# Clustered attention and two MLPs on one core: transposed keys and queries written straight into the score operands, two operand sets by parity

## The chip, the cores and the metric

One core of a Trainium2 chip runs the whole program. The metric is device time in microseconds (us) of one execution; the median of several runs counts. Five engines work side by side and wait for each other through semaphores: TensorE (PE; PEld is its weight load), VectorE (DVE), ScalarE (ACT), GpSimd (POOL), and SyncE (SP), whose queue issues every DMA here, in program order.

## The reference: what is computed

Two batches, eight heads, 768 tokens, head width 64, sixteen centroids per head. A query attends only to the keys that have the same nearest centroid:

```
q_assign = argmax(q_n @ c_n.T)          # per head; q_n, k_n, c_n are normalised
k_assign = argmax(k_n @ c_n.T)
mask   = q_assign[:, None] == k_assign[None, :]
scores = where(mask, scale * q @ k.T, -1e9)
attn   = softmax(scores);  y = attn @ v
x = y as (1536 tokens, 512)
x = (sigmoid(x @ w_gate) * (x @ w_val)) @ w_out      # F1 = 1536
x = relu(x @ w_in2)**2 @ w_out2                      # F2 = 2048
```

The MLP weights come as 64-bit floats and are decoded on the core into a high and a low float32 part.

## The kernel before

Every float32 number is used as a sum of a rounded high part (`hi`) and a rest (`lo`), because TensorE reads rounded operands. The heads are taken two at a time: eight pairs (2 batches by 4), numbered i = 0 to 7. A pair has 12 units: 2 heads (e), 2 halves of the queries (n), 3 blocks of 128 queries (j). So there are N = 96 units, and the main loop runs once per unit n: row maximum of the scores (DVE, L875), exponential (ACT, L896), six transposes of the probabilities of unit n-3 (PE, L776), their high part (ACT, L778) and low part (DVE, L784), the scores of unit n+1 (PE, L758), a third of the product with the values (PE, L794 and L795), and the normalisation of a unit's probabilities (POOL, L829). Engines run their queues in program order.

While the units of one pair run, `prep` makes the operands of the next. Its steps are spread over units by the tables `STEPS` and `SECOND_STEPS` (for pair 1): the key says at which unit of the pair before (0 to 11, negative ones in the pair before that) a step is written. `tk0`, `tk1`, `tq0`, `tq1` transpose half of the keys or queries of both heads (PE, L548) and split the result into `hi` and `lo`; `s0`, `s1`, `b0`, `b1`, `am`, `eq`, `oh`, `on` find the nearest centroids; `mk` makes 16 mask rows for the keys and 16 for the queries of each head; `ka`, `kb`, `qa`, `qb` are `stack`, which brings `hi` and `lo` of one head into the operand of the score product. A step's second part (ACT, DVE, POOL work on the PSUM result) is a "post" that is written early in the next unit.

The score product is two matmuls deep: Q·K = hi·hi + lo·hi in the first (both halves of the 128 rows are used), then hi·lo plus the mask rows in the second (64 + 16 = 80 rows). So a stacked operand needs copies of `hi` and `lo` in other partitions than they were made in, and copies across partitions are DMAs: three per head and tensor, twelve per pair, 192 KB each (L587 to L589). `hi_k`, `lo_k`, `hi_q`, `lo_q` of all pairs but pair 1 lie in pool `hl`, which has one buffer of each; pair 1 borrows a buffer of the attention's own `pt_hi` and `pt_lo`. For queries of pairs 1 to 7 ACT first copies the PSUM result (`full`, L555), then rounds it to `hi` (L556), and POOL subtracts to get `lo` (L557); for keys DVE subtracts straight from PSUM (L560).

The attention's output of a pair is moved across partitions too: two DMAs per head and half, four per half and pair (`x<-oc`, L804 and L805), then POOL adds (L813). After the last unit the MLPs run: blocks of matmuls L342 to L344 and L420, with the decoding of weights on DVE and ACT. Two weights are decoded early, during pairs 0 to 3, in the tile `spare` (`EARLY_PARTS` lists the units).

Of the kernel before, what the change touches and what calls it, by code (L numbers as in the profile page):

```python
# [29 lines left out]
    -9: ["tq0"],  # L30
    -8: ["tk0"],
    -7: ["tk1"],
    -6: ["tq1", "s0"],
    -5: ["load"],
    -4: ["b0"],
    -3: ["s1", "qa"],
    -2: ["ka"],
    -1: ["kb", "qb"],
    0: ["b1"],
    1: ["am"],  # L40
    3: ["eq"],
# [5 lines left out]
    -8: ["tk0", "load"],  # L47
# [3 lines left out]
    -2: ["qa"],  # L51
    -1: ["s1", "b0"],
    0: ["b1", "ka"],
    1: ["kb"],
    2: ["qb"],
    4: ["am"],
# [15 lines left out]
def cluster_attention_two_mlps(  # L72
# [239 lines left out]
    with tc.manual_schedule():  # L312
# [134 lines left out]
        with ExitStack() as ac:  # L447
# [3 lines left out]
            hl = pc.enter_context(tc.tile_pool(name="hl", bufs=1, side="right"))  # L451
# [9 lines left out]
            stk = sc.enter_context(tc.tile_pool(name="stk", bufs=3))  # L461
# [5 lines left out]
            nat_t, ahead = {}, {}  # L467
# [56 lines left out]

            Q, K, V = {}, {}, {}
            factor = {"q": scale, "k": 1.0}

            def prep(i):
# [4 lines left out]
                def transposes(nm, n):  # L533
                    def go():
                        if n == 0 and i == 1:

                            for t, x in ((hi_t, "pt_hi"), (lo_t, "pt_lo")):
                                if x not in ahead:
                                    ahead[x] = ptp.tile([P, NB, NH], F32R, name=x)
                                o = "kq".index(nm) * S  # L540
                                t[nm] = ahead[x].rearrange("p b n -> p (b n)")[:, o : o + S]
                        elif n == 0:
                            hi_t[nm] = hl.tile([P, S], F32R, name=f"hi_{nm}")
                            lo_t[nm] = hl.tile([P, S], F32R, name=f"lo_{nm}")
                        tr = ps_t.tile([P, NH], F32, name="t")
                        src = nat_t[i, nm]
                        for j in range(HB):
                            nc.tensor.transpose(tr[:, j * P : (j + 1) * P], src[:, n * HB + j].rearrange("p h d -> p (h d)"), ident)  # L548

                        def post():  # L550
                            sl = slice(n * NH, (n + 1) * NH)
                            hi, lo = hi_t[nm][:, sl], lo_t[nm][:, sl]
                            if nm == "q" and i > 0:
                                full = am.tile([P, NH], F32, name="full", bufs=1)
                                nc.scalar.activation(out=full, in_=tr, func=AF.Copy, scale=factor[nm])  # L555
                                nc.scalar.copy(hi, full)  # L556
                                nc.gpsimd.tensor_tensor(out=lo, in0=full, in1=f32(hi), op=ALU.subtract)  # L557
                            else:
                                nc.scalar.activation(out=hi, in_=tr, func=AF.Copy, scale=factor[nm])
                                nc.vector.scalar_tensor_tensor(  # L560
                                    out=lo, in0=tr, scalar=factor[nm], in1=f32(hi), op0=ALU.mult, op1=ALU.subtract
                                )

                        return post

                    return go

                def stack_tile(nm, e):
                    if i % 2 == 0 or e == 0:
                        return stk.tile([P, 2, S], F32R, name=f"st_{nm}")  # L570
                    if i < len(pairs) // 2:

                        return x_in[NG - 1][nm == "q"].rearrange("p k t -> p (k t)")[:, : 2 * S].rearrange("p (a s) -> p a s", a=2)
                    if "stk2" not in pools:
                        assert decoded[0] == EARLY and not any(x < N - UPP for x in decoding)
                        early_stack.close()
                        pools["stk2"] = sc.enter_context(tc.tile_pool(name="stk2", bufs=1))
                    return pools["stk2"].tile([P, 2, S], F32R, name=f"st_{nm}")

                def stack(nm, heads=(0, 1)):  # L580
                    def go():
                        for e in heads:
                            t = stack_tile(nm, e)
                            (Q if nm == "q" else K)[i, e] = t
                            t = f32(t)
                            hi, lo = (f32(x[nm][D * e : D * e + D]) for x in (hi_t, lo_t))
# [82 lines left out]
                def mask():  # L669
# [4 lines left out]
                    def post():  # L674
# [8 lines left out]
                        for e in range(0 if i > 0 else 1, 2):  # L683
                            for t, tensor in enumerate((K, Q)):
                                r = slice((2 * t + e) * NCL, (2 * t + e + 1) * NCL)
                                nc.sync.dma_start(out=f32(tensor[i, e][D : D + NCL, 1]), in_=f32(row[r]))
# [3 lines left out]
                if i == 0:  # L690
                    return [
                        transposes("k", 0),
                        transposes("k", 1),
                        transposes("q", 0),
                        transposes("q", 1),
                        stack("k", (0,)),
                        sims(0),
                        sims(1),
                        stack("q", (0,)),
                        back(0),  # L700
                        back(1),
                        argmax,
                        equal,
                        stack("k", (1,)),
                        stack("q", (1,)),
                        onehot,
                        one,
                        mask,
                    ]
# [10 lines left out]
                    "ka": stack("k", (0,)),  # L720
                    "kb": stack("k", (1,)),
                    "qa": stack("q", (0,)),
                    "qb": stack("q", (1,)),
# [26 lines left out]
            DEPTH = (2 * D, D + NCL)  # L750

            def scores(u):
# [3 lines left out]
                for a in range(2):  # L756
                    for m in range(2):
                        nc.tensor.matmul(  # L758
                            st[:, m, :NH],
                            Q[i, e][: DEPTH[a], a, c * P : (c + 1) * P],  # L760
                            K[i, e][: DEPTH[a], a, m * NH : (m + 1) * NH],
# [24 lines left out]
            def attend(i, e, n, third):  # L786
# [9 lines left out]
                if third == 2:  # L796

                    def post():
                        oc = sm.tile([P, NH], F32, name="oc", bufs=2)
# [33 lines left out]
            load(0, "v")  # L833

# [153 lines left out]
```

## Time and profile before

| | |
|---|---|
| median of 3 runs | 851.24 us (849.12 to 852.61) |
| the profiled execution's own time | 852.56 us |
| its span, first to last instruction | 850.8 us |
| mean granted TensorE clock | 0.986 of full speed |
| busy share of the span: PE, DVE, ACT, POOL | 96%, 73%, 53%, 25% |
| last row maximum of the attention (unit 95) starts at | 272.5 us |

The span lies 1.8 us below the time of the same execution; the profiled execution is 1.3 us above the median. "Busy" counts an instruction from its start to its end; PE's instructions overlap, so a busy PE need not be PE at its best.

### The profile page before, as it was taken

What the parts mean: (1) busy time and instruction counts of PE and PEld (TensorE: products, weight loads), DVE (VectorE), ACT (ScalarE), POOL (GpSimd) and SP (SyncE); (2) the same over time, 40 slices, a digit from 0 to 9 for tenths busy, and PEclk for the clock granted to TensorE, in tenths of its full rate; (3) what the DMA queues carried; (4) which work ended last, traced back from release to release, by engine and by line L of the source; (5) the groups of instructions that cost most, each with busy time, mean ns of one, the idle gap of its engine ahead of it and who ended that gap; (6) DMA issues with size and microseconds to landing.
All of it is one profiled execution on the core that took longest, in us unless ns stands there. A gap on an engine that the chain in (4) does not pass through costs nothing.

```text
span 850.8 us, 11707 instructions
## 1 busy us (share of the span) xinstructions
PE 815.1 (96%) x4069; PEld 695.2 (82%) x4069; DVE 622.0 (73%) x1129; ACT 449.5 (53%) x900; POOL 214.6 (25%) x339
## 2 busy tenths in 40 slices
PE   7697899998999999999999999999999999999998
PEld 5587898898989888788888888887878888888886
DVE  5697988898988567765687857796675788688533
ACT  7586888897888323442333213344645642642630
POOL 1567889897788300000000000000000000000000
PEclk9899999999999999999999999999999999999999
DMA  9764845855622212221211212111222212212012
GB/s 197 187 134 124 186 106 138 186 119 125 150 76 59 78 49 75 75 75 49 75 62 63 63 61 75 54 46 50 75 74 75 75 53 74 88 59 74 25 50 99
DMA packets 68107, 75.67 MB, mean 89 GB/s; under 512 B 29680, under 2 KB 56304, under 8 KB 68048
## 3 DMA queue, kind: packets, MB, share of 16 engines
q1 hardware_dynamic: 68048, 74.93, 33.2%
q8 instruction: 32, 0.52, 0.3%
q14 instruction: 27, 0.22, 0.1%
HBM read 45.12 MB, written 3.15 MB: 57 GB/s over the span
## 4 chain that ended last, share of the span: by engine, by line
PE 83%; DVE 5%; ACT 4%; POOL 2%; DMA 2%; issue 2%; SPq 1%; POOLq 0%; ACTq 0%; DVEq 0%
PE bank_b L420 16%; PE bank_a L343 12%; PE bank_a L344 12%; PE bank_a L342 12%; PE bank_a L420 9%; PE s L758 6%; PE t L776 6%; PE o L794 3%; PE o L795 3%; PE t L601 1%; DMA st_q<-lo_q 1%; DVE pt_lo L784 1%; POOL p L829 1%; PE t L548 1%; DMA x_lo<-pt_hi 1%
## 5 line engine op out<-in xcount | busy, mean ns | idle before, releaser
L344 PE MATMUL bank_a<-x_hi,w 128*128 128x512 f32 x480 | 188.5, 393 | 2.1 <-DVE w L230 2.1
L343 PE MATMUL bank_a<-x_lo,w 128*128 128x512 f32 x480 | 190.0, 396 | 0.4 <-POOL x_lo L824 0.4
L342 PE MATMUL bank_a<-x_hi,w 128*128 128x512 f32 x480 | 188.6, 393 | 0.0
L784 DVE TENSOR_TENSOR pt_lo<-t,pt_hi 128x384 fp32r<-128x384 f32 x192 | 97.3, 547 | 23.3 <-ACT pt_hi L778 22.5
L344 PEld LDWEIGHTS bank_a<-x_hi,w 128*128 128x128 f32 x480 | 90.5, 188 | 22.8 <-DVE w L230 2.5
L342 PEld LDWEIGHTS bank_a<-x_hi,w 128*128 128x128 f32 x480 | 90.5, 189 | 21.0
L343 PEld LDWEIGHTS bank_a<-x_lo,w 128*128 128x128 f32 x480 | 90.4, 188 | 20.7 <-POOL x_lo L824 0.8
L386 DVE TENSOR_TENSOR slo<-act,shi 128x512 fp32r<-128x512 f32 x84 | 57.4, 687 | 59.0 <-ACT shi L385 54.5
L829 POOL TENSOR_SCALAR p<-p,nm,ones 128x768 f32<-128x768 f32 x96 | 95.3, 993 | 19.5 <-DVE nm L828 13.1
L776 PE MATMUL t<-ident,p 128*128 128x128 f32 x576 | 83.8, 282 | 15.0 <-POOL lo_q L557 12.8
L875 DVE TENSOR_REDUCE nm<-s 128x1 f32<-128x768 f32 x96 | 90.9, 947 | 4.3 <-PE s L758 4.2
L896 ACT ACTIVATE p<-s,nm 128x768 f32<-128x768 f32 x96 | 88.3, 920 | 7.4 <-DVE nm L828 3.4
L778 ACT CAST pt_hi<-t 128x384 fp32r<-128x384 f32 x192 | 83.6, 488 | 16.3 <-PE t L776 8.7
L776 PEld LDWEIGHTS t<-ident,p 128*128 128x128 f32 x576 | 69.1, 144 | 22.5 <-POOL lo_q L557 13.8
L758 PE MATMUL s<-st_k,st_q 128*128 128x384 f32 (+1 forms) x336 | 81.9, 367 | 2.1 <-ACT p L896 1.1
L420 PE MATMUL bank_b<-wo,shi 128*128 128x512 f32 x256 | 79.3, 390 | 0.5 <-DVE wo L230 0.5
L385 ACT CAST shi<-act 128x512 fp32r<-128x512 f32 x84 | 51.2, 614 | 52.1 <-PE bank_b L420 27.1
L224 ACT CAST w<-wtop 128x512 fp32r<-128x512 f32 x38 | 23.7, 623 | 103.1 <-DVE wtop L242 103.1
L368 DVE TENSOR_TENSOR act<-bank_a,sg 128x512 f32<-128x512 f32 x36 | 24.9, 691 | 66.4 <-PE bank_a L344 60.4
L794 PE MATMUL o<-pt_hi,vt 128*128 128x384 f32 x192 | 66.7, 348 | 0.4 <-ACT oc L800 0.4
L795 PE MATMUL o<-pt_lo,vt 128*128 128x384 f32 x192 | 66.0, 344 | 0.0
L242 DVE SCALAR_TENSOR_TENSOR wtop<-wmag,wbody 128x512 f32<-128x512 f32 x66 | 45.3, 687 | 23.8 <-ACT wmag L210 21.8
(136 smaller groups left out, 1416.7 us busy)
## 6 DMA issues: line engine op xcount, KB each, us to landing
wraw<-in_moe_w_out_dram SPq DMA_DIRECT2D x28, 512.0 KB, 3.3
wraw<-in_moe_w_in_dram SPq DMA_DIRECT2D x16, 512.0 KB, 3.8
x<-oc SPq DMA_DIRECT2D x64, 96.0 KB, 2.7
wraw<-in_moe_w_gate_dram SPq DMA_DIRECT2D x11, 512.0 KB, 3.7
wraw<-in_moe_w_val_dram SPq DMA_DIRECT2D x11, 512.0 KB, 3.6
st_k<-hi_k SPq DMA_DIRECT2D x26, 192.0 KB, 4.1
st_q<-hi_q SPq DMA_DIRECT2D x26, 192.0 KB, 4.1
nat_v<-in_v_dram SPq DMA_DIRECT2D x8, 384.0 KB, 3.2
```

Source lines behind the costliest of these rows:

```text
L342: nc.tensor.matmul(bk, w[:, 0, ks], mov_hi[:, kk], start=(kk == 0), stop=False)
L343: nc.tensor.matmul(bk, w[:, 0, ks], mov_lo[:, kk], start=False, stop=False)
L344: nc.tensor.matmul(bk, w[:, 1, ks], mov_hi[:, kk], start=False, stop=(kk == KD - 1))
L420: nc.tensor.matmul(bk, st, mv, start=(first and n == 0), stop=(last and n == 2))
L758: nc.tensor.matmul(st[:, m, :NH], Q[i, e][: DEPTH[a], a, c * P : (c + 1) * P], K[i, e][: DEPTH[a], a, m * NH : (m + 1) * NH], start=(a == ...
L776: nc.tensor.transpose(tp[:, m, :], Pt[u][:, c * P : (c + 1) * P], ident)
L784: nc.vector.tensor_tensor(out=lo, in0=tp, in1=f32(hi), op=ALU.subtract)
L794: nc.tensor.matmul(o, vt, hi[:, c, :], start=(c == 0), stop=False)
L795: nc.tensor.matmul(o, vt, lo[:, c, :], start=False, stop=(c == NB - 1))
L829: nc.gpsimd.tensor_scalar(out=p, in0=p, scalar1=nm[:, 3:4], scalar2=ones, op0=ALU.mult, op1=ALU.mult)
L875: nc.vector.tensor_reduce(out=nms[n][:, 0:1], in_=st[n][:, :, :NH], axis=AX.XY, op=ALU.max, negate=True)
L896: nc.scalar.activation(out=e.rearrange("p (m n) -> p m n", m=2), in_=st.pop(n)[:, :, :NH], func=AF.Exp, bias=nms[n][:, 0:1], accum_out=nms ...
```

## The change

Transposed keys and queries are written into the operand of head 0 at once; what head 1 and the second halves need is copied from there. The operands are fixed tiles, `stacks[nm, e, x]`, two sets (x = i % 2) instead of rotating buffers. For head 1 the rows are mirrored: its own data stay in the upper 64 partitions, and its mask rows go to partitions 48 to 63 with zeros below (rows 0 to 47, written once), so its second matmul is 128 rows deep instead of 80. Only the low part of the queries has a tile of its own, one buffer for all pairs: a piece of `x_in[2][0]` (`x_hi_65` in listings), from pair 6 on a tile `lo_q` in a new pool.

```
 STEPS = {
-    -9: ["tq0"],  -8: ["tk0"],  -7: ["tk1"],  -6: ["tq1", "s0"],  -5: ["load"],  -4: ["b0"],
-    -3: ["s1", "qa"],  -2: ["ka"],  -1: ["kb", "qb"],  0: ["b1"],  1: ["am"],
+    -8: ["tq0"],  -7: ["tk0"],  -6: ["tk1"],  -5: ["tq1", "s0"],  -3: ["b0", "load"],  -2: ["s1"],
+    -1: ["kb"],  0: ["qb", "b1"],  1: ["am"],  2: ["ka", "qa"],
     3: ["eq"], 6: ["oh", "on"], 7: ["mk"],
...
-    -8: ["tk0", "load"],
+    -8: ["tk0"],
...
-    0: ["b1", "ka"],
+    0: ["b1", "load"],
...
-    4: ["am"],
+    4: ["am", "ka", "qa"],
...
+            stacks[nm, e, x] = stk.tile([P, 2, S], F32R, ...)      # k and q, 2 heads, 2 parities
...
-                        elif n == 0:
-                            hi_t[nm] = hl.tile([P, S], F32R, name=f"hi_{nm}")
-                            lo_t[nm] = hl.tile([P, S], F32R, name=f"lo_{nm}")
+                        if n == 0:
+                            a = stacks[nm, 0, i % 2]
+                            hi_t[nm], lo_t[nm] = a[:, 0], a[:, 1]
+                            if nm == "q":
+                                lo_t[nm] = low_tile()
...
-                            if nm == "q" and i > 0:
-                                full = am.tile([P, NH], F32, name="full", bufs=1)
-                                nc.scalar.activation(out=full, in_=tr, func=AF.Copy, scale=factor[nm])
-                                nc.scalar.copy(hi, full)
-                                nc.gpsimd.tensor_tensor(out=lo, in0=full, in1=f32(hi), op=ALU.subtract)
-                            else:
...
+                            nc.scalar.activation(out=hi, in_=tr, func=AF.Copy, scale=factor[nm])
+                            nc.vector.scalar_tensor_tensor(out=lo, in0=tr, scalar=factor[nm], in1=f32(hi), ...)
+                            if nm == "q":
+                                copy(stacks[nm, 0, i % 2][:D, 1, sl], hi[:D])          # POOL, 64 x 384
+                            if i == 0:
+                                own = stacks[nm, 1, 0][D:, :, sl]
+                                if nm == "q":
+                                    nc.scalar.activation(out=own, in_=tr[D:, None, :].to_broadcast([D, 2, NH]), ...)
+                                else:
+                                    copy(own, stacks[nm, 0, 0][D:, :, sl])
...
-                            nc.sync.dma_start(out=t[:D, 0], in_=hi)
-                            nc.sync.dma_start(out=t[D:, 0], in_=lo if nm == "q" else hi)
-                            nc.sync.dma_start(out=t[:D, 1], in_=hi if nm == "q" else lo)
+                        if e == 0:
+                            nc.sync.dma_start(out=a[D:, 0], in_=f32(lo_t[nm])[:D] if nm == "q" else a[:D, 0])
+                            return
+                        if i > 0:
+                            own = a[D:, 0:1].to_broadcast([D, 2, S]) if nm == "q" else a[D:]
+                            nc.sync.dma_start(out=b[D:], in_=own)
+                        other = f32(lo_t[nm])[D:] if nm == "q" else b[D:, 0] if i == 0 else a[D:, 0]
+                        nc.sync.dma_start(out=b[:D, 0], in_=other)
...
-            DEPTH = (2 * D, D + NCL)
+            DEPTH = ((2 * D, D + NCL), (2 * D, 2 * D))
...
-                            xs[n] = [sm.tile([P, NH], F32, name=f"x{t}", bufs=2) for t in range(2)]
-                        nc.sync.dma_start(out=xs[n][0][own], in_=oc[own])
+                            xs[n] = [oc, sm.tile([P, NH], F32, name="x", bufs=2)]
                         nc.sync.dma_start(out=xs[n][1][own], in_=oc[other])
+                        if e == 1:
+                            nc.sync.dma_start(out=xs[n][0][own], in_=oc[own])
...
+            for nm in "kq":
+                for x in range(2):
+                    nc.gpsimd.memset(stacks[nm, 1, x][: D - NCL, 1].bitcast(I32), 0)
```

What that makes of SP's queue for one pair in the middle (pair 5; `hi_q`, `lo_q`, `hi_k`, `lo_k` are the split transposes, `oc` the attention's output). Before, head 0 (the same six follow for head 1, keys first, then the copies of `oc`):

```order
L587 DMA st_q<-hi_q 64x768
L588 DMA st_q<-lo_q 64x768
L589 DMA st_q<-hi_q 64x768
L587 DMA st_k<-hi_k 64x768
L588 DMA st_k<-hi_k 64x768
L589 DMA st_k<-lo_k 64x768
```

In the changed kernel the same place (`st_k_142` and `st_q_144` are head 0 of this parity, `st_k_143` and `st_q_145` head 1, `x_hi_65` the queries' low part), both heads:

```order
L600 DMA st_k_143<-st_k_142 64x1536
L602 DMA st_k_143<-st_k_142 64x768
L819 DMA x<-oc_2172 64x384
L600 DMA st_q_145<-st_q_144 64x2x768
L602 DMA st_q_145<-x_hi_65 64x768
L596 DMA st_k_142<-st_k_142 64x768
L596 DMA st_q_144<-x_hi_65 64x768
L819 DMA x<-oc_2279 64x384
L821 DMA oc_2052<-oc_2279 64x384
```

Twelve copies of 192 KB became six, two of them of 384 KB; head 1 comes first, since the copies into head 0 (L596) overwrite what head 1's copies read.

DVE's queue at the start, where pair 0's nearest centroids are found (`mx`, `eq`, `m`, `oh`) while pair 1 is split (L560). Before:

```order
L639 TENSOR_REDUCE mx<-tot 128x24
L560 SCALAR_TENSOR_TENSOR pt_lo<-t,pt_hi 128x384
L646 TENSOR_TENSOR eq<-tot,mx 128x384
L649 TENSOR_TENSOR eq<-eq,first 128x384
L560 SCALAR_TENSOR_TENSOR pt_lo<-t,pt_hi 128x384
L656 TENSOR_REDUCE m_313<-eq 128x24
```

In the changed kernel:

```order
L652 TENSOR_REDUCE mx<-tot 128x24
L557 SCALAR_TENSOR_TENSOR x_hi_65<-t,st_q_144 128x384
L659 TENSOR_TENSOR eq<-tot,mx 128x384
L662 TENSOR_TENSOR eq<-eq,first 128x384
L557 SCALAR_TENSOR_TENSOR st_k_142<-t,st_k_142 128x384
L669 TENSOR_REDUCE m_306<-eq 128x24
```

The subtraction ahead of `eq` was one of keys into a borrowed tile; now it is one of queries into the single low tile.

## Rows read from the trace of the kernel before

**Rows 1.** Busy time in stretches: us, each engine's busy us (instructions), clock, DMA share, GB/s.
```profile
30.20:73.61 43.41, 31.83 (x195) 28.89 (x193) 31.15 (x65) 27.22 (x62) 23.60 (x34) 0.92 0.67 159
73.61:106.55 32.94, 30.74 (x202) 29.36 (x201) 29.93 (x61) 27.27 (x64) 28.12 (x41) 0.95 0.62 139
139.37:170.67 31.30, 29.40 (x202) 27.86 (x201) 27.17 (x58) 26.93 (x64) 27.33 (x41) 1.00 0.65 145
170.67:199.64 28.97, 28.73 (x200) 27.61 (x198) 26.49 (x55) 24.98 (x60) 24.88 (x38) 1.00 0.67 148
201.97:230.58 28.61, 28.61 (x189) 27.70 (x188) 25.58 (x53) 25.51 (x61) 23.66 (x37) 0.94 0.55 123
700.00:800.00 100.00, 100.00 (x440) 82.31 (x439) 78.90 (x134) 44.58 (x77) 0.00 (x0) 1.00 0.22 69
```

**Rows 2.** Who waited for whom: us in total, times, longest.
```profile
PE t L776 <- POOL lo_q L557: 12.8, 5, 4.3
ACT hi_q L556 <- DMA st_q<-hi_q: 11.6, 4, 4.6
ACT pt_hi L778 <- DMA x_lo<-pt_hi: 7.0, 1, 7.0
```

**Rows 3.** Timeline around one hand-over (pair 6 ends its copies, pair 7 begins): start, us.
```profile
184.39 0.95 PE L758 MATMUL s<-st_k,st_q 128*128 128x384 f32 x4
188.14 0.48 ACT L800 COPY oc<-o 128x384 f32<-128x384 f32 x1
195.98 0.94 SPq L589 DMA_DIRECT2D st_q<-hi_q  x1
200.10 0.51 ACT L556 CAST hi_q<-full 128x384 fp32r<-128x384 f32 x1 [2.58 <-DMA st_q<-hi_q]
201.73 0.92 PE L776 MATMUL t<-ident,p 128*128 128x128 f32 x6 [2.33 <-POOL lo_q L557]
```

**Rows 4.** Busy time and clock just after another hand-over (columns as in rows 1).
```profile
108.00:110.00 2.00, 2.00 (x10) 1.90 (x9) 1.82 (x4) 1.36 (x3) 1.84 (x4) 0.50 0.00 0
```

**Rows 5.** Groups of instructions by line and shape: count, busy us, mean ns, idle before.
```profile
L557 POOL TENSOR_TENSOR lo_q<-full,hi_q 128x384 fp32r<-128x384 f32 x12 | 12.1, 1004 | 8.5 <-ACT hi_q L556 8.3
L560 DVE SCALAR_TENSOR_TENSOR lo_k<-t,hi_k 128x384 fp32r<-128x384 f32 x14 | 7.6, 549 | 2.7 <-ACT hi_k L559 2.7
L737 POOL TENSOR_SCALAR vt<-nat_v 128x384 fp32r<-128x384 f32 x16 | 8.2, 513 | 1.2
L556 ACT CAST hi_q<-full 128x384 fp32r<-128x384 f32 x12 | 6.2, 513 | 14.2 <-DMA st_q<-hi_q 11.6 <-DMA x_lo<-hi_q 2.4
L795 PE MATMUL o<-pt_lo,vt 128*128 128x384 f32 x192 | 66.0, 344 | 0.0
L758 PE MATMUL s<-st_k,st_q 80*128 80x384 f32 x168 | 44.2, 345 | 1.0 <-issue 0.7 <-ACT st_q L678 0.4
```

**Rows 6.** Issue to landing, of the 192 KB copies L587, then of the 384 KB loads of `nat_v`.
```profile
DMA to landing us min/median/max: 2.6/4.1/6.4
...
DMA to landing us min/median/max: 3.0/3.2/5.8
```

**Rows 7.** The stretch in which the twelve copies of one pair move (columns as in rows 1).
```profile
186.60:200.00 13.40, 12.79 (x88) 12.32 (x87) 11.82 (x25) 10.07 (x24) 10.39 (x17) 1.00 1.00 217
```

**Rows 8.** Timeline of the start: last centroid product, first `eq`, first row maximum.
```profile
10.11 0.37 PE L601 MATMUL t<-lo_q,cen 128*128 128x384 f32 x1
13.38 0.55 DVE L646 TENSOR_TENSOR eq<-tot,mx 128x384 f32<-128x384 f32 x1
20.05 0.96 DVE L875 TENSOR_REDUCE nm<-s 128x1 f32<-128x768 f32 x1 [3.31 <-PE s L758]
```

**Rows 9.** Timeline of the long stall in pair 0, and the row maximum of unit 8 behind it.
```profile
36.08 0.43 DVE L235 TENSOR_SCALAR spare<-spare 128x512 int32<-128x512 int32 x1 [3.49 <-DMA spare<-in_moe_w_gate_dram]
39.87 0.86 ACT L778 CAST pt_hi<-t 128x384 fp32r<-128x384 f32 x2 [6.95 <-DMA x_lo<-pt_hi]
47.35 0.94 DVE L875 TENSOR_REDUCE nm<-s 128x1 f32<-128x768 f32 x1
```

More of the change, by code (lines that the diff above doesn't have):

```diff
@@ L29 @@
 STEPS = {
[L30 to L39, printed above, removed]
+    -8: ["tq0"],
+    -7: ["tk0"],
+    -6: ["tk1"],
+    -5: ["tq1", "s0"],
+    -3: ["b0", "load"],
+    -2: ["s1"],
+    -1: ["kb"],
+    0: ["qb", "b1"],
     1: ["am"],
+    2: ["ka", "qa"],
     3: ["eq"],
@@ L460, in cluster_attention_two_mlps @@
             sc = ac.enter_context(ExitStack())
-            stk = sc.enter_context(tc.tile_pool(name="stk", bufs=3))
+            stacks = {}
+            for x in range(2):
+                stk = pc.enter_context(tc.tile_pool(name="stk0", bufs=1, side="right")) if x == 0 else sc.enter_context(
+                    tc.tile_pool(name="stk1", bufs=1)
+                )
+                for nm in "kq":
+                    for e in range(2):
+                        stacks[nm, e, x] = stk.tile([P, 2, S], F32R, name=f"st_{nm}{e}{x}")
             early_stack = sc.enter_context(ExitStack())
@@ L466, in cluster_attention_two_mlps @@
             pairs = [(b, hp) for b in range(B) for hp in range(NPAIR)]
-            nat_t, ahead = {}, {}
+            nat_t = {}
             def load(i, nms):
@@ L523, in centroid_prep, with copy @@
                     nc.vector.tensor_tensor(out=lo, in0=ctv[r, :, e, :], in1=f32(hi), op=ALU.subtract)
+            def copy(out, src):
+                nc.gpsimd.tensor_scalar(out=out, in0=f32(src), scalar1=1.0, scalar2=1.0, op0=ALU.mult, op1=ALU.mult)
             Q, K, V = {}, {}, {}
@@ L578, in stack_tile, with stack @@
-                    return pools["stk2"].tile([P, 2, S], F32R, name=f"st_{nm}")
-                def stack(nm, heads=(0, 1)):
+                        pools["hl"] = sc.enter_context(tc.tile_pool(name="hl", bufs=1))
+                    return pools["hl"].tile([P, S], F32R, name="lo_q")
+                def stack(nm, e):
                     def go():
[L582 to L586, printed above, removed]
-                            nc.sync.dma_start(out=t[:D, 0], in_=hi)
-                            nc.sync.dma_start(out=t[D:, 0], in_=lo if nm == "q" else hi)
-                            nc.sync.dma_start(out=t[:D, 1], in_=hi if nm == "q" else lo)
+                        a, b = (f32(stacks[nm, x, i % 2]) for x in range(2))
+                        (Q if nm == "q" else K)[i, e] = stacks[nm, e, i % 2]
+                        if e == 0:
[6 more added lines that the diff above has]
+                        nc.sync.dma_start(out=b[:D, 0], in_=other)
@@ L685, in post @@
                                 r = slice((2 * t + e) * NCL, (2 * t + e + 1) * NCL)
-                                nc.sync.dma_start(out=f32(tensor[i, e][D : D + NCL, 1]), in_=f32(row[r]))
+                                at = D - NCL if e else D
+                                nc.sync.dma_start(out=f32(tensor[i, e][at : at + NCL, 1]), in_=f32(row[r]))
                     return post
@@ L833, in cluster_attention_two_mlps @@
             load(0, "v")
+            for nm in "kq":
+                for x in range(2):
+                    nc.gpsimd.memset(stacks[nm, 1, x][: D - NCL, 1].bitcast(I32), 0)
             warm = ps_o.tile([P, NH], F32, name="o")
```

54 lines of the change are left out of this document (24 added, 30 removed).

## The prediction

> **What bounds the kernel now.** I read the busy time by stretches first. In the MLPs PE is busy for all of 100 us at full clock [rows 1], and the change issues nothing there, so that part can only start earlier. In the attention I cut the time at the row maxima of single units (L875). Twelve units with the next pair's preparation in them, from unit 53 at 170.67 to the moment at which unit 65 would have started had nothing waited (201.97 less the 2.33 of the wait), take 28.97 us, with PE busy for 28.73 and DVE for 26.49 [rows 1]. That is the clean period, bound by PE. The real ones are longer: 43.41 for units 5 to 17, 32.94 for 17 to 29 (29 to 41 is alike), 31.30 for 41 to 53 (53 to 65 is alike), and the last, 65 to 77, has no wait but a clock of 0.94 [rows 1].
>
> The waits say why. PE's transposes (L776) wait five times, 12.8 us in all, for POOL's low part of the queries, and behind that ACT's `hi_q` waits for a DMA that still reads `hi_q` for the pair before [rows 2]. The hand-over at 196 to 202 us shows the chain: the last of twelve copies is issued at 195.98, only at 200.10 may ACT overwrite `hi_q`, and at 201.73 PE goes on, after 2.33 us [rows 3]. The copies cannot come sooner: while they move, the DMA engines are busy all the time, at 217 GB/s [rows 7]. In pair 0 the same happens through the borrowed tile: ACT's `pt_hi` waits 6.95 us for a copy out of it [rows 9].
>
> A wait costs more than itself. Behind the one ahead of unit 29, in which PE stood still, the clock is at half speed, 1.2 instead of 2.4 GHz [rows 4]. The last period puts a price on it: 6% of 28.61 us, 1.7 us [rows 1].
>
> **The change, part by part.**
>
> *The hand-over.* `hi` and the keys' `lo` now go into operands that change with parity. Their readers of two pairs ago are score products that PE has issued ahead of the new transposes, so nothing is late there. What is left in one buffer is the queries' low part: DVE may write it for pair i+1 only when `qa` of pair i, its last reader, has landed. `qa` waits for the first `qb` copy (it overwrites what that reads). SP does not wait for the unit under which a step is written, only for semaphores, so on the times of the old hand-over: `kb` may go when the scores at 184.39 are done, 185.3; two issues at 0.94; then the copy of `oc`, made by ACT at 188.14 to 188.62, so the first `qb` copy starts at 189.6 [rows 3]. A copy lands 4.1 us after its issue, at most 6.4; twice the size over all partitions took 3.2, at most 5.8 [rows 6]. So `qb` lands at 193.7 and `qa` at 197.8. DVE would write the low part behind the row maximum of unit 65, at 199.64 + 0.96 [rows 1, 8] = 200.6: 2.8 us of slack, so I cost it at nothing. With 6.4 twice, `qa` lands at 202.4 and DVE waits 1.8. Queued behind that DVE write are the low parts L784, which free the PSUM buffers PE needs. The next copies of `oc` stand behind `qa` on SP and can go from 194.7; POOL's add of them (L813) is written more than a unit after ACT makes `oc`, so I cost this at nothing too (rival three is the case that it isn't).
>
> So each hand-over falls back to the clean period: 32.94 - 28.97 = 4.0 us for units 17 to 29, as much for 29 to 41, 2.3 for 41 to 53, as much for 53 to 65, and the 1.7 of clock in the last [rows 1]: 14.3 us.
>
> *Queries split by DVE.* POOL loses 14 subtractions of about 1.0 us and gets 14 half-height copies, bounded by its one-input pass over as many columns, 0.51; ACT loses 14 roundings of 0.51 [rows 5]. Both have slack, so no gain. DVE gets 14 subtractions of 0.55, 7.7 us [rows 5]. In the clean period it has 2.5 us free against 1.1 more per pair [rows 1], but they fall in units 5 and 8, next to `oh` and `on` in unit 6. Between 0 and 7.7 I take the middle, 3.9 us lost.
>
> The Trainium skill (Perfetto Trace Analysis, section Optimizing Scalar/DVE Operations) says that where DVE is saturated it may make sense to give work to Scalar or GpSimd; the change does the reverse. By that rule the whole 7.7 us would be paid and the sum below would be 842; rival two is that case.
>
> *Head 1's second product 128 deep instead of 80.* The 80-row one takes 345 ns, a 128-row one in the same place of a pair (L795) 344 [rows 5]: nothing.
>
> *Fewer transfers.* 1.5 MB instead of 2.3 per pair, 6 issues instead of 12. Outside the chains above it is hidden either way. One copy of `oc` less per half and pair is hidden too.
>
> *The start.* Here the single low tile costs. Pair 1's queries are split while pair 0's copies still read it. Two extra ACT writes of 768 columns (twice 0.51 each [rows 5]) come in; one lies on the path, so the last centroid product ends at 11.5 instead of 10.5 [rows 8]. Then three copies are issued, the third at 13.4, landing at 16.0 to 17.5 [rows 3, 6]. Behind that, with a 0.55 subtraction, `eq` starts at 16.6 to 18.1 instead of 13.38 [rows 8]: 3.2 to 4.7 us later, and the first scores with it. I take 3.6. The four POOL memsets are done before POOL has anything else to do.
>
> Then pair 2's low part, in unit 5, waits for pair 1's `qa`. Unit 5 starts at 30.20 + 3.6, so DVE asks at 34.8. SP issues mask rows at about 24, then 0.1 + 0.8 MB of loads, 0.5 of weights, 1.0 of copies up to the first `qb`: 2.4 MB at 217 GB/s [rows 7] is 11 us, 35; `qa` lands 2.6 to 4.1 later, 37.6 to 39.1. So DVE waits 2.8 to 4.3; I take 4.0, and 1.6 for the clock behind it. Against this stands the old stall: units 5 to 8 took 47.35 - 30.20 = 17.2 us [rows 1, 9] where three clean units take 7.2; about 1 us of the excess is decoding that stays, so 9.0 goes. The wait of 4.3 at unit 17 [rows 2] goes as well; its clock is in the 14.3. Sum to unit 17: -3.6 - 5.6 + 9.0 + 4.3 = 4.1 us gained.
>
> **Sum.** 4.1 + 14.3 - 3.9 = 14.5 us off the profiled execution's 852.6: 838.1. That execution is 1.3 us above its median, well inside the range; I say 838.
>
> **Rivals.**
> 1. *The start comes clean too.* If the DMA queue is nearly empty when pair 1's copies go, their landing at the minimum of 2.6 [rows 6] makes both waits small: 5.6 us more, and with DVE's charge hidden, 9.5. That gives 829 to 833. For it: less to move. Against: the engines were full throughout such a stretch [rows 7].
> 2. *DVE paces the pair.* All 7.7 us are paid, and as much again if the low parts L784 come late enough to hold PE through the PSUM buffers: 842 to 850. For it: in units 5 to 7 everything is nearly full. Against: 2.5 us free per clean period [rows 1].
> 3. *Another wait takes the hand-over's place*, say the POOL add of the output behind SP's queue: start gained, periods as before, 849 to 852, no change.
> 4. *The single low tile on DVE, slower.* If `qb` and `qa` land later than anything seen here, DVE waits w at each of five hand-overs, and the clock falls behind each. The gain of 14.5 is used up at w = 2.9 without the clock, that is with both landings at 7.0 us. At 8 us each (twice the median) w = 5.0 and with 1.6 of clock the time is 838 + 33 = 871. For it: a 64-partition copy of 384 KB is nowhere in the trace. Against: 217 GB/s moves it in 1.8 us.
>
> **How the numbers follow.** The forecast 0.60 (833 to 845), rivals 0.13, 0.12, 0.08, 0.07. The range reaches from rival 1 to the end of rivals 2 and 3, 829 to 851. About 0.5%, 4.3 us, is what a measurement can tell from no change, so faster means below 847.0: the forecast, rival 1 and 0.07 of rival 2, 0.80. The rest of rival 2 and rival 3 are 0.13; rival 4 is 0.07.
>
> **What the profile after would show.** No wait of PE's transposes on POOL's low part; `hi` written by ACT without a DMA wait in pairs 3 to 7; periods of 29 to 30 us; one DVE wait on a copy out of the low tile ahead of the first `eq` and one in unit 5. Wrong if DVE's low-tile subtraction waits for a DMA in later pairs, if the periods stay at 31 us or more with DVE busy throughout, or if the MLPs do not start earlier by what the attention saves.

## The result, and the profile after

| | before | after |
|---|---|---|
| median on the same chip | 851.68 us (849.12 to 852.61, 4 runs) | 857.52 us (857.24 to 859.68, 4 runs) |
| ratio, 95% interval | | 1.0079 [1.0051, 1.0107] |
| the profiled execution: own time, span | 852.56, 850.8 us | 857.28, 855.5 us |
| last row maximum (unit 95) starts at | 272.51 us | 275.59 us |

The change made the kernel slower by 0.8%; the time lies outside the forecast's range. The stretches of [rows 1] in the changed kernel, units 5 to 17, 17 to 29, 41 to 53, 53 to 65 and 65 to 77, then the same stretch of the MLPs:

```profile
32.19:72.16 39.97, 31.45 (x195) 28.47 (x193) 32.43 (x66) 26.91 (x62) 22.20 (x32) 0.91 0.49 112
72.16:108.36 36.20, 30.66 (x202) 27.88 (x201) 29.91 (x64) 26.59 (x61) 28.30 (x42) 1.00 0.51 118
140.08:172.24 32.16, 30.20 (x202) 27.98 (x201) 28.08 (x60) 26.23 (x61) 27.07 (x42) 1.00 0.48 111
172.24:203.85 31.61, 29.89 (x202) 27.95 (x201) 27.95 (x60) 26.26 (x62) 24.99 (x40) 1.00 0.49 114
203.85:235.31 31.46, 29.99 (x203) 28.00 (x201) 27.96 (x60) 26.27 (x63) 25.14 (x40) 1.00 0.39 89
700.00:800.00 100.00, 100.00 (x440) 82.39 (x439) 80.18 (x136) 43.64 (x75) 0.00 (x0) 1.00 0.22 69
```

The MLPs' matmuls are as before; the loss lies ahead of them. The later periods are not 29 us but 31.5 to 32, and PE is busy for only 30 of them. The waits, for [rows 2]:

```profile
ACT oc L815 <- POOL x_lo L840: 11.0, 7, 1.7
DVE x_hi L557 <- DMA st_q<-x_hi: 9.0, 2, 6.2
PE t L551 <- DVE x_hi L557: 9.1, 2, 6.9
PE o L809 <- ACT oc L815: 7.3, 7, 2.0
```

No wait of [rows 2] is left, as forecast: PE's transposes of the probabilities no longer wait for the queries' low part. Two new waits stand in their place. The first comes seven times, once per pair but the first. Around unit 60 (start, us, then what the engine waited for):

```profile
190.88 0.95 DVE L894 TENSOR_REDUCE nm<-s 128x1 f32<-128x768 f32 x1
191.55 1.14 POOL L840 TENSOR_TENSOR x_lo<-oc,x_hi 128x128 fp32r<-128x128 f32 x2
192.73 0.48 ACT L815 COPY oc<-o 128x384 f32<-128x384 f32 x1 [1.54 <-POOL x_lo L840]
193.26 0.44 PE L809 MATMUL o<-pt_hi,vt 128*128 128x384 f32 x1 [0.82 <-ACT oc L815]
194.56 0.95 DVE L894 TENSOR_REDUCE nm<-s 128x1 f32<-128x768 f32 x1
```

In this program ACT may not copy the output of head 0 into `oc` before POOL has read the last low part (`x_lo`) of the pair before out of the same buffer; PE waits behind ACT for its only PSUM buffer of `o`. The unit takes 3.68 us; unit 60 of the kernel before took 2.10. The seventh time is the hand-over to the MLPs, where PE stands longest; the first MLP matmul comes 7.86 us after the start of unit 95's row maximum, 4.65 us in the kernel before:

```profile
279.69 0.69 PE L809 MATMUL o<-pt_hi,vt 128*128 128x384 f32 x1 [2.03 <-ACT oc L815]
```

The second wait is that of the single low tile, at two places (unit 5 and unit 17), and behind the first the clock is at half speed:

```profile
36.71 0.46 SPq L596 DMA_DIRECT2D st_q<-x_hi  x1
39.38 0.56 DVE L557 SCALAR_TENSOR_TENSOR x_hi<-t,st_q 128x384 fp32r<-128x384 f32 x1 [6.24 <-DMA st_q<-x_hi]
39.99 0.90 PE L551 MATMUL t<-ident,nat_k 128*128 128x128 f32 x3 [6.86 <-DVE x_hi L557]
...
75.90 0.56 DVE L557 SCALAR_TENSOR_TENSOR x_hi<-t,st_q 128x384 fp32r<-128x384 f32 x1 [2.79 <-DMA st_q<-x_hi]
```

```profile
40.00:42.00 2.00, 2.00 (x10) 1.92 (x11) 2.00 (x5) 0.92 (x2) 1.24 (x2) 0.50 0.02 4
```

These are the queries of pairs 2 and 3; from pair 4 on DVE never waits for the low tile.

### The profile page after: what moved, and what is told of

It reads as the page before. It is cut to its first block, busy times and chain, and to the rows that moved or that the text cites. A ratio compares the mean times of both kernels' runs of the same rounds, so it can differ in the third digit from the quotient of the medians.

```text
span 855.5 us, 11621 instructions
## 1 busy us (share of the span) xinstructions
PE 816.7 (95%) x4069; PEld 693.1 (81%) x4069; DVE 626.2 (73%) x1143; ACT 446.6 (52%) x888; POOL 213.6 (25%) x347
## 4 chain that ended last, share of the span: by engine, by line
PE 72%; DVE 13%; POOL 5%; ACT 4%; issue 3%; DMA 2%; SPq 0%; DVEq 0%; POOLq 0%; ACTq 0%
PE bank_b L418 16%; PE bank_a L341 12%; PE bank_a L342 12%; PE bank_a L340 12%; PE bank_a L418 9%; DVE pt_lo L799 3%; PE s L773 3%; PE t L791 3%; DVE nm L894 3%; POOL p L845 3%; PE o L809 2%; PE o L810 2%; POOL x_lo L840 1%; DMA st_q<-st_q 1%; PE t L614 1%
## 5 line engine op out<-in xcount | busy, mean ns | idle before, releaser
L773 PE MATMUL s<-st_k,st_q 128*128 128x384 f32 (+1 forms) x384 | 93.7, 367 | 1.5 <-ACT p L915 0.8
L773 PEld LDWEIGHTS s<-st_k,st_q 128*128 128x128 f32 (+1 forms) x384 | 64.9, 196 | 3.2 <-ACT p L915 1.8
```

The costliest lines, as they stand in the source:

```text
L773: nc.tensor.matmul(st[:, m, :NH], Q[i, e][: DEPTH[e][a], a, c * P : (c + 1) * P], K[i, e][: DEPTH[e][a], a, m * NH : (m + 1) * NH], start= ...
```

## The experiments

The theory: the loss is the wait for `oc`. In the kernel before, `oc` was free as soon as two DMAs had read it, and POOL worked on tiles of their own (`x0`, `x1`); in the changed kernel the `oc` of head 0 is itself POOL's sum tile, held until the last low part a pair later, still with two buffers. The rivals: (A) DVE's added subtractions pace the pairs, and the wait only shows who is late; (B) the loss is in the start, through the single low tile. All medians stand beside runs of the kernel before on the same chip. The experiments ran in four groups (e1 to e4; e7, e8, e9 and e11; e10, e12, e13 and e16; e6, e17 and e18), in which the kernel before took 850.81, 852.31, 852.05 and 853.41 us; across groups the ratio to it is the fairer figure. "Units 53 to 64" is the time between those two row maxima, 26.98 us in the kernel before.

### The buffer of oc

**e1_oc3**, a third buffer for head 0:

```
-                        oc = sm.tile([P, NH], F32, name=f"oc{e}", bufs=2)
+                        oc = sm.tile([P, NH], F32, name=f"oc{e}", bufs=3 - e)
```

> The changed kernel with one edit: three instead of two buffers for the attention output of head 0 (oc0), which the change made into a tile that POOL adds into and reads until the end of the pair. Theory (the buffer wait: ACT's copy into oc0 waits for POOL's last low part of the pair before, 1.7 us seven times, and PE behind it 2.0 us): those waits vanish, units 24, 36, 48, 60, 72 and 84 fall from 3.7 to about 1.9 us, and the MLPs are handed over 1.6 us sooner; 6 x 1.8 + 1.6 + some clock = 13 us less than the changed kernel, about 843 to 846. Rival A (DVE's added subtractions pace the pair; the wait for POOL is only where the lateness shows): the time goes to other waits and the kernel stays at 854 to 858. Rival B (the loss is in the start: the single low tile): also 854 or more.

Measured 847.17 us, ratio 0.9942 [0.9919, 0.9965]: 10.4 below the changed kernel's 857.52; by the ratios the gain is 11.7 us, and the two profiled executions lie 12.7 apart. At the same unit 60 the copy no longer waits, and POOL's last low part runs after it:

```profile
185.57 0.48 ACT L815 COPY oc<-o 128x384 f32<-128x384 f32 x1
186.01 1.15 POOL L840 TENSOR_TENSOR x_lo<-oc,x_hi 128x128 fp32r<-128x128 f32 x2
```

Units 24, 36, 48, 60, 72 and 84 take 1.9 to 2.1 us, 3.5 to 3.8 in the changed kernel, and the first MLP matmul comes 3.2 us sooner behind unit 95. The theory holds; the gain is a little under the 13 expected, and the unit behind each is longer again by 0.1 to 0.3 (61: 2.80 instead of 2.58).

**e3_after_oldoc**, the changed kernel with the oc part undone:

```
-                            xs[n] = [oc, sm.tile([P, NH], F32, name="x", bufs=2)]
+                            xs[n] = [sm.tile([P, NH], F32, name=f"x{t}", bufs=2) for t in range(2)]
+                        nc.sync.dma_start(out=xs[n][0][own], in_=oc[own])
```

> The changed kernel with the oc part undone: two sum tiles of their own and four copies of the output per pair and half, as in the kernel before; the operands stay as changed. Theory (the buffer wait): the loss goes, as with the third buffer: 843 to 847, within 2 us of that kernel if copies are hidden. If the added copies in SP's queue, between those of the operands, are paid: 2 to 6 us above the kernel with the third buffer. Rival A or B: 854 to 859.

848.64 us, 0.9966 [0.9952, 0.9979]: the loss goes here too, and the one more copy per half and pair costs 1.5 us by the medians, within the spread of the runs. So the new operands alone are worth 0.34%.

**e2_before_oc**, the other way round: the kernel before with the oc part alone (the same edit with + and - exchanged).

> The kernel before with the oc part of the change alone: head 0's output copy is itself the sum tile, two buffers, one copy less per half and pair; everything else as before. Theory (the buffer wait): a wait of ACT's oc copy for POOL's last low part at the end of each pair, about 1.8 us six or seven times, on top of the waits at the hand-over: 857 to 865. Should the old stall, five units later, give some back, 853 to 857. Rival A or B (the oc part costs nothing, the loss is elsewhere): 848 to 853, like the kernel before, or a little less for the fewer copies.

853.77 us, 1.0024 [1.0011, 1.0037], in the second span (853 to 857), below the theory's first. The trace shows two things that nearly cancel:

```profile
ACT oc L800 <- POOL x_lo L825: 11.7, 7, 2.0
PE o L794 <- ACT oc L800: 8.1, 7, 2.0
PE t L776 <- POOL lo_q L557: 4.3, 1, 4.3
```

```profile
188.55 0.48 ACT L800 COPY oc<-o 128x384 f32<-128x384 f32 x1 [1.60 <-POOL x_lo L825]
193.76 1.39 SPq L589 DMA_DIRECT2D st_q<-hi_q  x1
197.96 0.51 ACT L556 CAST hi_q<-full 128x384 fp32r<-128x384 f32 x1 [0.38 <-DMA st_q<-hi_q]
```

The wait for `oc` is there seven times, as in the changed kernel. But the old hand-over waits, five in [rows 2], are down to one. From unit 53 to the last operand copy it is 24.57 us instead of 25.31 (fewer `oc` copies stand ahead of it in SP's queue), and unit 64 comes 1.65 us later through the new wait: 2.4 us more room, and the 2.33 of [rows 3] are covered.

**e11_before_oc_sums** takes most of the new wait out of that kernel (0.7 us is left at unit 48, 0.4 at unit 84), by ending the second half's sums a unit earlier:

```
-SUMS = [[5, 6, 8], [6, 8, 9]]
+SUMS = [[5, 6, 8], [6, 7, 8]]
```

> The kernel before with the oc part of the change and POOL's last low part of a pair one unit earlier, so that oc0 is free in time; operands, step table and split as before. The run of the oc part alone showed two things that cancel: the new wait of 1.8 us at units 24, 36, ..., and the old hand-over waits (units 28, 40, 52, 64) gone. Theory (one cause for both: the copies of the operands come sooner because fewer oc copies stand ahead of them, by about 1.2 us; the rest of the old wait was hidden by the new one): without the new wait about half of the old ones comes back, 843 to 848. Rival (the fewer copies cure the hand-over by themselves): 839 to 842. Rival (the new wait is not from the buffer): 852 to 854.

845.49 us, 0.9908 [0.9878, 0.9938], within the theory's span. PE's hand-over waits are back in part, 6.4 us in three instead of 12.8 in five. So the oc part, with its buffer free in time, is worth 0.9% on the old operands, more than the new operands alone.

### The low tile and what stood behind it

**e4_oc3_low2**: e1_oc3 and a second low tile (the other piece of `x_in`, and two tiles in the new pool).

```
-                        return x_in[NG - 1][0].rearrange("p k t -> p (k t)")[:, :S]
+                        return x_in[NG - 1][i % 2].rearrange("p k t -> p (k t)")[:, :S]
...
-                    return pools["hl"].tile([P, S], F32R, name="lo_q")
+                    return pools["hl"].tile([P, S], F32R, name=f"lo_q{i % 2}")
```

> The changed kernel with the third buffer for oc0 and, besides, two low tiles for the queries, by parity, instead of one. The single low tile shows two waits of DVE on a copy out of it in the changed kernel, 9.0 us in all: ahead of the first eq (pair 1) and in unit 5 (pair 2). Theory: both vanish, the first row maximum starts at about 20 us instead of 21.9, and unit 5 takes about 5 us instead of 9.2: 5 us (3 to 8) below the kernel with the third buffer alone, so 836 to 841. Rival (the start is bound by the loads and copies themselves, the wait on the low tile only shows it): within 1.5 us of the kernel with the third buffer alone.

841.93 us, 0.9880 [0.9854, 0.9905]: 5.2 below e1_oc3, the size expected. Unit 5 falls from 9.00 to 2.84 us and unit 17 from 4.19 to 2.34. The other half of the theory fails: the start comes no earlier (unit 0 at 23.11 us, 21.83 in e1_oc3), DVE never waited for a copy there. And unit 18 now takes 8.33 us instead of 4.39. SP, POOL, DVE and PE around it:

```profile
61.85 0.60 SPq L602 DMA_DIRECT2D st_q<-x_hi  x1
66.46 0.46 SPq L596 DMA_DIRECT2D st_k<-st_k  x1
67.63 0.46 SPq L596 DMA_DIRECT2D st_q<-x_hi  x1
68.78 0.59 SPq L821 DMA_DIRECT2D oc<-oc  x1
72.86 0.99 POOL L829 TENSOR_TENSOR oc<-oc,x 128x384 f32<-128x384 f32 x1 [4.48 <-DMA oc<-oc]
75.61 0.17 DVE L844 RECIPROCAL nm<-nm 128x1 f32<-128x1 f32 x1 [4.78 <-POOL nm L929]
76.39 1.51 PE L791 MATMUL t<-ident,p 128*128 128x128 f32 x6 [4.53 <-DVE pt_lo L799]
```

The copy of `oc` is written behind the copies into head 0's operands (L596). SP holds these back 4.0 us, behind the copies that read what they overwrite; POOL stands at its addition; behind it on POOL is the normalisation, for that DVE waits, and for DVE PE.

**e6_low2**: the second low tile without the third buffer.

> The changed kernel with the two low tiles alone (oc0 keeps its two buffers). With the third buffer the second tile was worth 5.2 us by the medians. If the low tile's waits are a cost of their own: 850 to 854. If the wait for oc0 hides them (or the wait of POOL in unit 18 takes their place in full): 855 to 858.

854.46 us, 1.0009 [0.9985, 1.0032], half a microsecond above the first span: 3.1 below the changed kernel by the medians, 6.0 by the ratios (the chips differ); unit 95 starts 4.1 us earlier. Unit 5 falls from 9.18 to 2.85 and unit 17 from 5.21 to 2.35, but unit 18 rises from 4.39 to 8.89. The low tile's waits are a cost of their own; about half of what the trace gains there goes back to POOL's wait.

**e9_sums**: two low tiles, and POOL's sums at other units instead of the third buffer (`SUMS = [[7, 7, 8], [6, 7, 8]]`).

> The changed kernel with two low tiles by parity, and with POOL's sums of a pair at other units: for the first half the addition two units later, for the second half the last low part one unit earlier (instead of a third buffer for oc0). Theory: the early last part frees oc0 in time (no ACT wait for POOL's low part, as with the third buffer), and the late addition takes away the wait that the run with two low tiles showed in unit 18, where POOL waited 4.5 us for the copy oc<-oc behind the operands' copies in SP's queue: 841.9 - 4 = about 838 (835.5 to 839.5), unit 18 at 3 to 4.5 us instead of 8.3. Rival: POOL is late there anyway, its work only moves: 841 to 843.

842.00 us, 0.9867 [0.9834, 0.9900], no better than e4_oc3_low2. Unit 18 is down to 3.48, as the theory had it, but between units 20 and 95 it takes 186.8 us against 183.6. Nearly all of that, 2.9 us, lies behind unit 77: units 80 to 84 and 92 are longer, that is units 8 to 10 of the last two pairs, and DVE waits there for POOL's normalisation (1.2 us in unit 80, 1.7 in unit 92); the crowded sums as the reason fit, but up to unit 77 they cost 0.3 us. So both sides were half right. **e12_late0** keeps the third buffer and the old sums and delays the first half of pair 0 alone:

```
-                                at = n + SUMS[w[2]][t] if w[0] < len(pairs) - 1 else n + (3 if end else 6)
+                                at = n + ([7, 8, 9][t] if w[0] == 0 == w[2] else SUMS[w[2]][t]) if w[0] < len(pairs) - 1 else n + (3 if end else 6)
```

> The changed kernel with the third buffer for oc0, the two low tiles, POOL's sums at their old units, and only pair 0's first half added two units later. Theory: the 4.5 us wait of unit 18 goes (18: 3 to 4.5 us), and the sums that e9_sums had crowded into units 8 to 10 of every pair are spread again, where that run lost 3.1 us between units 20 and 95 against the run with the third buffer: 836 to 839. Rival (both differences are lost to the clock behind unit 92 or in the MLPs, as in that run): 840 to 843.

837.86 us (836.85 to 837.94), 0.9833 [0.9807, 0.9858]: 4.1 below e4_oc3_low2 (4.0 by the ratios). Its stretches, units 5 to 17, 17 to 29, 41 to 53 and 53 to 65:

```profile
32.07:65.91 33.84, 31.02 (x195) 27.83 (x193) 32.37 (x66) 26.97 (x61) 22.10 (x32) 0.95 0.57 134
65.91:97.30 31.39, 29.81 (x202) 27.90 (x201) 31.12 (x64) 26.44 (x60) 28.03 (x42) 1.00 0.58 134
127.65:158.46 30.81, 29.77 (x202) 27.98 (x201) 28.32 (x60) 26.37 (x60) 27.14 (x42) 1.00 0.50 116
158.46:188.72 30.26, 29.50 (x202) 28.00 (x201) 28.24 (x59) 26.41 (x62) 25.08 (x40) 1.00 0.52 119
```

All three waits are gone; from unit 41 on a period still takes 1.3 to 1.8 us more than the 28.97 of [rows 1].

### The rest: step table and DVE

**e7_steps** and **e8_poolq** each undo one part in e9_sums: the first puts `tq0`, `tk0`, `tk1`, `tq1` with `s0` back to -9, -8, -7, -6; the second gives the queries of pairs 1 to 7 back to ACT (`full`, `hi`) and POOL (`lo`). **e10_steps_poolq** has both.

> As e9_sums, and the transposes and splits of pairs 2 to 7 one unit earlier, as in the kernel before (tq0 at -9 to tq1 with s0 at -6). In the run with the third buffer a period still takes 30.25 us (units 53 to 65) against 28.97 clean, longer in units 55, 56 and 59. Theory S (the step table: tq1 and s0 now share a unit with the mask rows): 1.2 us per period for 5 to 6 periods, 6 to 7 us below e9_sums. Rival D (DVE's added subtractions, wherever they stand): within 2 us of e9_sums.

844.16 us, 0.9891 [0.9858, 0.9923]: 2.2 above e9_sums, not the 6 to 7 below of theory S.

> As e9_sums, but the queries of pairs 1 to 7 split as in the kernel before: ACT copies and rounds, POOL subtracts; DVE gets none of it. Theory D (DVE's 14 subtractions of 0.55 us are what the periods lost): 4 to 8 us below e9_sums. Theory S (the place of the steps): within 2 us of e9_sums. If POOL's longer path (1.0 us instead of 0.55, behind the normalisations) holds PE up: slower than e9_sums by 2 or more.

849.34 us, 0.9966 [0.9946, 0.9986]: 7.3 above e9_sums, the third case.

> As e9_sums, with both the earlier steps and the queries split by ACT and POOL, that is the whole preparation as before on the changed operands. Each alone was slower than e9_sums (844.2 and 849.3 against 842.0). If the two only help together: units 53 to 64 at 27 to 27.5 us, 836 to 839. If POOL's subtraction is paid wherever it stands: 846 to 850, units 53 to 64 over 28.5.

852.91 us, 1.0009 [0.9993, 1.0025]. None of them helps. The split on ACT and POOL costs 7.3 us here (e8_poolq, whose lines follow): units 53 to 64 take 29.48 us (28.38 in e9_sums), and PE waits more often for what comes behind POOL (in e9_sums, 4.2 us in 11 waits):

```profile
DVE nm L850 <- POOL nm L935: 25.4, 38, 2.3
PE t L797 <- DVE pt_lo L805: 10.1, 20, 1.7
```

These three stand on the crowded sums, which load POOL where the split does. The step table alone was therefore tried again on e12_late0, **e13_late0_steps**:

```
-    -8: ["tq0"],  -7: ["tk0"],  -6: ["tk1"],  -5: ["tq1", "s0"],
+    -9: ["tq0"],  -8: ["tk0"],  -7: ["tk1"],  -6: ["tq1", "s0"],
```

> As e12_late0, with the transposes and splits of pairs 2 to 7 one unit earlier, as in the kernel before. Units 53 to 64 took 26.98 us in the kernel before and 28.39 with the third buffer; with the earlier steps on crowded sums 28.12. Theory S (the step table is what costs 1.4 us per pair, and the crowded sums hid that): units 53 to 64 at 27.0 to 27.4, 5 us below e12_late0, 831 to 835. Theory D (DVE's two more subtractions per pair cost it wherever they are): 28.0 to 28.4, within 2 us of e12_late0.

835.89 us (835.70 to 836.90), 0.9815 [0.9789, 0.9841], the lowest median: 2.0 below e12_late0, where theory S wanted 5. Units 53 to 64 take 27.58 us (28.40 in e12_late0), but unit 64 itself 2.32 (1.86). In **e18_pair2_late** pair 2 keeps the later steps:

> As e13_late0_steps, with pair 2's transposes and splits left at the later units of the change. In that run unit 4 takes 4.96 us against 2.81 with the later steps, PE waits there for the load of pair 2's queries. Theory: 2 us come back, 833.5 to 834.5. Rival (the wait only moves to the following units): 835.5 to 836.5.

836.08 us, 0.9800 [0.9770, 0.9829]. The medians say the rival, the ratios 1.3 us of gain, within the intervals: undecided. Unit 4 falls from 4.96 to 2.80 us, units 7 and 8 take 0.8 more, and in the profiled executions unit 95 starts 1.4 us earlier.

DVE's subtraction was cut short in **e17_short_split** (e13_late0_steps with `c = slice(0, 32 if nm == "q" and 2 <= i < len(pairs) - 2 else NH)` on its operands) and put alone into the kernel before in **e16_before_dveq**.

> As e13_late0_steps, but for pairs 2 to 5 DVE subtracts only 32 of the 384 columns of each half of the queries' low part (the rest of the low part keeps older values, so that part of the computation is left out). That takes about 0.4 us of DVE away twice per pair, in four pairs. Theory D (DVE's added subtraction is paid in full): 3.2 us below e13_late0_steps, 832 to 833.5, periods of pairs 2 to 4 shorter by 0.8. As forecast (half of it): 834 to 834.8. Theory of no charge: within 0.8 us of e13_late0_steps.

837.09 us, 0.9806 [0.9779, 0.9834]: no gain that the medians or the ratios can tell. Eight subtractions fall from 0.55 to 0.18 us, 2.9 us of DVE; in the profiled executions units 5 to 77 take 183.9 us, 185.0 in e13_late0_steps, so little more than a third of it shows, and in the two full periods of units 29 to 53 only 0.1 us: 0.36 us gained in unit 43 is lost again in unit 44. Units 41 to 53 of e13_late0_steps, then of e17_short_split (they start at 129.55 and 128.50):

```profile
129.55:160.06 30.51, 30.02 (x202) 27.79 (x201) 28.13 (x59) 26.69 (x62) 27.55 (x43) 1.00 0.51 117
```

```profile
128.50:159.02 30.52, 29.98 (x202) 27.78 (x201) 27.83 (x59) 26.75 (x62) 27.52 (x43) 1.00 0.52 117
```

> The kernel before with one part of the change, the queries of pairs 1 to 7 split by DVE straight from PSUM; nothing else. If DVE's 14 subtractions are paid (half of 7.7 us as forecast, up to all of it): 2 to 8 us slower than before, 853 to 859. If they are free or shorten the hand-over (0.55 us of DVE behind ACT instead of a copy, a rounding and 1.0 us of POOL): 846 to 851.

856.84 us, 1.0055 [1.0039, 1.0072], 4.8 slower, in the span of a paid subtraction. The trace does not show DVE's time alone, though: the old hand-over is still there, and now DVE's queue stands in it. As at unit 64, ACT waits for the copy out of `hi_q`, DVE for ACT, and behind DVE's subtraction stand the low parts and PE.

```profile
206.29 0.49 ACT L553 ACTIVATE hi_q<-t 128x384 fp32r<-128x384 f32 x1 [3.05 <-DMA st_q<-hi_q]
206.82 0.56 DVE L554 SCALAR_TENSOR_TENSOR lo_q<-t,hi_q 128x384 fp32r<-128x384 f32 x1 [1.84 <-ACT hi_q L553]
207.36 1.00 DVE L778 TENSOR_TENSOR pt_lo<-t,pt_hi 128x384 fp32r<-128x384 f32 x2
207.43 0.55 PE L548 MATMUL t<-ident,nat_k 128*128 128x128 f32 x3 [1.99 <-DVE lo_q L554]
```

Over all five hand-overs PE waits 14.4 us there instead of 12.8 (longer at four, a little shorter at unit 64). Between units 5 and 95 PE stands idle 2.5 us more in all and is busy 2.2 us more; the granted clock is 0.96 and 0.95 in units 41 to 53 and 53 to 65, where it was 1.00, and 1.00 in units 65 to 77, where it was 0.94. How much of the 4.8 us is DVE's own time, this run can't tell.

## Why the prediction was wrong

What each stretch gave, in us gained against the kernel before, by the row maxima of the profiled executions:

| stretch | forecast | changed kernel | e12_late0 |
|---|---|---|---|
| start to unit 5 | -3.6 | -2.0 | -1.9 |
| units 5 to 8 | 9.0 - 5.6 = 3.4 | -1.0 | 5.3 |
| units 8 to 16 | 0 | -0.1 | -0.3 |
| units 16 to 18 | 4.3 | 1.8 | 4.7 |
| units 18 to 77 | 14.3 - 3.9 = 10.4 | -1.5 | 5.7 |
| units 77 to 95 | 0 | -0.2 | 1.2 |
| unit 95 to the end | 0 | -1.6 | 0.0 |
| sum (by the spans) | 14.5 | -4.7 | 14.6 |

The row of unit 95 to the end mixes two things. The hand-over to the MLPs costs the changed kernel 3.2 us, but its profiled execution had a granted clock of 1.00 between 500 and 600 us, where those of the kernel before and of e12_late0 had 0.98.

- **The step that failed: "One copy of `oc` less per half and pair is hidden too", and the next copies and POOL's add of them costed "at nothing".** The forecast looked at when the addition may start, not at how long the tile is now held. With two buffers ACT stands 1.5 us at the same place of each pair, and the unit and the one behind it take 1.3 to 1.7 more; five times in units 18 to 77 (7.1 us, nearly all of the 7.2 between the last two columns), once more in units 84 and 85 (1.4), and at the hand-over to the MLPs (3.2). That is 11.7 us in all, and the third buffer takes out 10.4 by the medians, 11.7 by the ratios. So the loss is the wait for this buffer. Rival three named the neighbourhood (POOL's add behind SP's queue), but gave it 849 to 852. In its own form it exists too: 4.1 us at unit 18 (e4_oc3_low2 against e12_late0), once the waits ahead of it are gone.
- **The start and the single low tile.** The tile does hold DVE up, but not where the first part of it was put: ahead of the first `eq` the last copy out of it landed at 15.18 us, before DVE came to the subtraction at 15.30, and unit 0 came 1.9 us late, not 3.6. In unit 5 the wait is 6.2 us (forecast 4.0, at most 4.3), and there is one of 2.8 at unit 17, where the forecast had only a gain. The hand-overs to pairs 4 to 7 are free of it, so the slack held there. Rival four came at one of its five hand-overs, that of unit 17: the head-1 copies issued between 62.7 and 66.5 us landed 7.2 to 8.5 us later, beyond the 6.4 of [rows 6]. The old stall was valued at 9.0 us; with both waits gone units 5 to 8 still take 11.86 us (e12_late0) against 17.15, so it was worth 5.3.
- **The hand-over: right in mechanism, too large in size.** `hi` by parity ends the waits of [rows 2]. But the clean period of 28.97 us, read from one period behind a stall, is not reached: 30.3 to 30.8 in e12_late0. The earlier steps give back 0.3 to 0.8 of it. For the rest, 0.5 to 1.5 us per pair, the measure itself was too short. In [rows 1] PE is already busy for 29.40 us at full clock in units 41 to 53, and the old operands with most of their waits gone reach 28.97 only once (e11_before_oc_sums, units 41 to 53, 53 to 65 and 65 to 77):

```profile
135.93:166.44 30.51, 29.96 (x202) 27.74 (x201) 27.11 (x57) 27.21 (x65) 27.09 (x40) 1.00 0.64 143
166.44:196.86 30.42, 29.62 (x202) 27.86 (x201) 27.27 (x57) 26.96 (x64) 26.86 (x41) 1.00 0.63 144
196.86:225.73 28.87, 28.76 (x200) 27.61 (x198) 27.28 (x57) 26.20 (x62) 25.42 (x39) 1.00 0.56 124
```

Why a period takes 28.9 or 30.5 us stays open; that the engines other than PE catch up during a stall, so that the period behind it is short, was only argued. And half of the old hand-over waits (12.8 to 6.4 us) goes without the new operands, by fewer `oc` copies and an earlier last sum (e11_before_oc_sums).

- **DVE's 3.9 us.** The charge is not shown. The whole is not paid on the changed operands: with 2.9 us of the subtractions gone, 1.1 us at most shows (e17_short_split), so less than the half that was charged, within the noise of the runs. On the old operands the same subtractions came with 4.8 us, waits and clock included (e16_before_dveq). And the opposite move is worse: with DVE the busiest engine but PE, at 28 of 30 us, handing its work to ACT and POOL cost 7.3 us (e8_poolq). The rule of the Trainium skill (Perfetto Trace Analysis, section Optimizing Scalar/DVE Operations), by which the sum was 842, speaks of a saturated DVE and says that the move may make sense; here it did not. The same section of the Trainium skill cautions that moving work between GpSimd and DVE might not help. That agrees with the 7.3 us.
- **Nothing for the deeper product and the fewer operand copies.** No trace contradicts it, and no run took either out alone. POOL's half-height copies take 524 ns, the bound was 0.51 us.

That e12_late0 lands on the forecast of 838 is partly chance: the old stall and the periods were overvalued by 3.7 and 4.7 us, and the waits it lacks were charged 5.6 where they cost 19.4 (the span of 855.5 less 836.1).

## What to carry to other kernels

When an edit saves a copy by letting one tile serve as two, follow the tile to its last reader and ask what is written into the same buffer one round later; a buffer count that fitted the short life may be one too few for the long one. Cost each part of a change by itself: here one part was worth 0.9% and looked like a loss of 0.2% until its buffer was free in time. A wait taken out shows the next one in the same queue, so after each fix the unit that became longer is read next.

## What was not expected of the hardware

- SP can take three times as long to issue one copy as another, with no wait shown: `x<-oc` at 63.93 in the changed kernel took 1.81 us (DMA share 0.96 from 62 to 66 us), at 75.04 it took 0.59 (0.79 from 75 to 76.5). Full DMA engines are not the whole reason: the four issues of operand copies between 62.69 and 67.06 took 0.51 to 0.62, and in the kernel before `x<-oc` at 173.89 took 1.40 with a share of 0.24 (173.5 to 175.5).
- The first scores of pair 0 found either level of the clock: from 19 to 22 us the granted clock was 1.00 in e12_late0, 0.54 in e4_oc3_low2 and 0.51 in e9_sums, whose units 0 came 1.2 and 0.4 us later (23.11 and 22.37 against 21.95).
- In the MLPs, between 500 and 600 us, each of these traces has PE busy for 97.9 of 100 us, but the clock there was 1.00 in some executions (the changed kernel, e4_oc3_low2) and 0.98 in others (before, e9_sums, e12_late0). e9_sums ended its attention 2.1 us ahead of e4_oc3_low2 and had the same span, 841.2 and 841.1: a difference of 2 us between single executions can be the clock's alone.
